# Attention's tiled products of a unit side by side, its transposes behind them; keys ahead of queries; routing and first-slot steps moved

## The chip, the cores and the metric

One core of one Trainium2 chip. The time is device microseconds of one execution of the whole program. Before the change three executions took 1027.92, 1023.63 and 1026.13 us, a median of 1026.13 us.

## What is computed

```python
# 1. chunked attention: 4 batches, 8 heads, 768 positions, head_dim 64; chunks of 32 queries
for c in range(24):
    k_full = concat(mem_k (8), k[c*32-16 : c*32+40])       # window clipped at the ends
    a = softmax(q[c*32 : c*32+32] @ k_full.T / 8)
    out[c*32 : c*32+32] = a @ v_full
# 2. mixture of 8 experts, the best one for each of the 3072 tokens (d = 512, f = 1024)
logits = x @ w_gate + modality_bias[modality_id];  e = argmax(logits);  gate = softmax(logits)[e]
out = gate * (relu(x @ w1[e]) @ w2[e])
# 3. a dense block: elu(x @ w_in) @ w_out, 512 -> 2048 -> 512
```

All in float32. Products of parts 2 and 3 are made of three products of split numbers (high and low parts).

## The kernel before, in words

The instructions of each engine stand in the order in which the Python program emits them (a manual schedule), so each engine is a queue: what stands first and waits holds up all behind it. PE is the matrix engine (TensorE), PEld its weight loads, DVE the VectorE, ACT the ScalarE, POOL the GpSimd, SP the engine that issues most transfers.

**Attention** (L54 to L515). An item is one batch and four heads (`items`, 8 of them); a unit is a third of an item, eight chunks (`units`, 24 of them, u = 3 ix + G). `A.run` (L442) emits for each unit: `sc(u, 0)` and `sc(u, 1)`, the scores of two groups of four chunks, in 32-column tiles (`tile_position`, L278); `sm(u)`, maximum and subtraction on DVE; `exp(u)` on ACT; `tr(u - 1)`, four 128 x 128 transposes of the unit before, and ACT's copy of them; `pv(u - 2)`, the products with v, again in 32-column tiles (L321), into one bank `ps_v`, from which DVE normalizes into x (L329). Beside them `step(i)` pops from `pend` the transposes that prepare the next item: `k_step` (three transposes, copies by ACT and DVE into `kbd`) and `q_step` (three transposes of `rl`, one copy by ACT into `qT`); `rl` is made by `relay` from the loaded q, on ACT up to item 3 and on POOL after. Three PSUM banks (`ps_t`) serve all transposes in turn. `load_v` and `load_qk` (SP) are issued at the first unit of an item; the halo of v is copied by POOL (`copy_v`).

The gate runs one batch behind: `gate_x` (eight transposes of x and two ACT copies), `gate_s` (x to the DRAM tensor xs, issued by POOL), `gate_l` (tiled products), `gate_t` (two transposes, a sum on DVE), `gate_e`, `gate_p`, `gate_r`, `gate_o` (choice of expert and ranks). `at(u, place, ...)` hangs them on places 0 to 5 of a unit; `side(u, place)` emits them. x and the staging of the memory's values (`repeat_v`, tensor mvd) share SBUF.

**Routing and slot 0.** The tokens of an expert are cut into slots of up to 384. Slot 0 needs batches 0 and 1 alone: `count`, `place`, `tokens(0)`, `gather(0)` (three indirect transfers issued by POOL), `scale` (ACT), `xT` (transposes). `M.first` (L891) runs slot 0's eight steps of `L1` (12 products) and, two steps later, `L2` (12 products), n = 2 to 9, with three places each, on which `program` hangs the last gates, `bases` (DVE), `slots` (POOL; it fills the register tile `reg`: which expert each slot has, how many slots there are), `tokens(1)`, `gather(1)` and `columns`. `split_w` makes high and low parts of a quarter of a pair of weight blocks (ACT casts, DVE subtracts); `load_w` brings a pair into one of three raw buffers. `M.run` (L910) then goes through slots 1 to 7 with PE as its pace, the rest of the slots follow under conditions, and `M2.run` is part 3.

Of the kernel before, what the change touches and what calls it, by code (L numbers as in the profile page):

```python
# [53 lines left out]
class Attention:  # L54
# [162 lines left out]
    def make_bias(self):  # L217

        nc, const, NT = self.nc, self.const, self.NT
        self.bias = self.rk.tile([128, NT, E], FP32, name="bias")  # L220
        tmp = const.tile([128, NT, E], FP32, name="btmp")
        mr = const.tile([NT, 128], FP32, name="mr")
        nc.vector.tensor_copy(out=mr, in_=self.mi[:, :, 0])
        mf = self.ps_t.tile([128, NT], FP32, name="ps_qk")
        nc.tensor.transpose(mf, mr, self.ident[0:NT, 0:NT])
        for m in range(2):
            m0 = const.tile([128, NT], FP32, name=f"m{m}")
            nc.vector.tensor_scalar(out=m0, in0=mf, scalar1=float(m), scalar2=None, op0=ALU.is_equal)
            o = self.bias if m == 0 else tmp
            nc.vector.tensor_tensor(out=o, in0=m0.unsqueeze(2).to_broadcast([128, NT, E]), in1=self.mb[:, m].unsqueeze(1).to_broadcast([128, NT, E]), op=ALU.mult)  # L230
        nc.vector.tensor_tensor(out=self.bias, in0=self.bias, in1=tmp, op=ALU.add)
# [26 lines left out]
    def tsteps(self, ix):  # L258
        steps = []
        for i in range(2):  # L260
            for j in range(2):
                steps.append(lambda i=i, j=j: self.k_step(ix, i, j))
                steps.append(lambda i=i, j=j: self.q_step(ix, i, j))
        return steps
# [177 lines left out]
    def run(self, more):  # L442
# [6 lines left out]
        def at(u, place, f, *a):  # L449
            todo.setdefault((u, place), []).append(lambda: f(*a))  # L450
# [5 lines left out]
        for b in range(self.B - 1):  # L456
            u0 = 6 * b + 6
            for G in range(3):
                at(u0 + G, 3, self.gate_x, b, G)
                at(u0 + G, 3, self.gate_s, b, G)  # L460
                at(u0 + G, 5, self.gate_l, b, G)
                at(u0 + G + 1, 2, self.gate_t, b, G)
# [10 lines left out]
        for u in range(N):  # L473
            ix, G = self.units[u]
            pops = [((0, 0, 0), (0, 0, 0), (3, 3, 2)), ((1, 1, 1), (1, 1, 1), (1, 1, 0))][ix > 0][G]
# [11 lines left out]
            if G == (2 if ix == 0 else 0) and ix + 1 < NI:  # L487
                self.relay(ix + 1, self.nc.scalar if ix < 3 else self.nc.gpsimd)
                pend = self.tsteps(ix + 1)
            self.sc(u, 0)  # L490
            side(u, 0)
            step(0)
            self.sc(u, 1)
            side(u, 1)
            if u:
                self.tr(u - 1)
            self.sm(u)
            side(u, 2)
            if u > 1:
                self.pv(u - 2)  # L500
            side(u, 3)
            step(1)
            self.exp(u)
# [5 lines left out]
            if u == 4:  # L509
                self.tables()  # L510
            if u == 5:
                self.make_bias()
# [33 lines left out]
class Routing:  # L546
# [139 lines left out]
    def slots(self):  # L686
# [34 lines left out]
        past(g1, base)  # L721
        TT(out=g1, in0=g1, in1=g2, op=ALU.subtract)
        self.g = g1
        eng.tensor_copy(out=reg[:, 2 * NSMAX:2 * NSMAX + 1], in_=end[:, 1, E - 1:E])
        eng.tensor_copy(out=reg[:, 2 * NSMAX + 1:], in_=base[:, 1, 0:1])
# [46 lines left out]
class Moe:  # L772
# [118 lines left out]
    def first(self, left):  # L891
# [6 lines left out]
        for n in range(LAG, NF + LAG):  # L898
# [5 lines left out]
            if n < 6:  # L904
                for i in range(2):
                    self.split_w(0, n // 2 + 1, 2 * (n % 2) + i)
# [252 lines left out]
def program(ctx, tc, q, k, v, mem_k, mem_v, mid, wg, mbias, w1, w2, w_in, w_out, out):  # L1159
# [11 lines left out]
    with ExitStack() as c2:  # L1171
        late, c4, c5, c6 = [ExitStack() for _ in range(4)]
        with tc.manual_schedule(engines=ORDER):
# [18 lines left out]
            def rest():  # L1192
# [4 lines left out]
                M.load_w(0, 3)  # L1197
# [14 lines left out]
                (N - 1, 2): [*[(M.split_w, 0, 1, i) for i in range(2)], (M.L1, 0, 0)],  # L1212
# [12 lines left out]
                (6, 0): [(rt.tokens, 1), (M.gather, 1), (rt.others, 2)],  # L1225
                (6, 2): [(rt.columns,)],
# [3 lines left out]
                (8, 2): [*[(M.xT, 1, kc) for kc in range(2, KC)]],  # L1230
# [81 lines left out]
```

## Time and profile before

| | us |
|---|---|
| median of three executions | 1026.13 |
| the profiled execution, its own time | 1027.93 |
| its span, first to last instruction | 1025.0 |
| PE busy | 976.8 (95% of the span) |
| DVE, ACT, POOL busy | 557.1, 426.8, 212.1 |
| mean granted clock of TensorE | 0.99 |

The rows below are from the page of the profile and from queries of its trace. Times in them are us from the start of the span unless ns stands there. A line number is that of the kernel before. Matmul ends are modelled, so durations of products overlap; the distance from start to start is what tells PE's pace.

### The profile page before, as it was taken

What the parts mean: (1) busy time and instruction counts of PE and PEld (TensorE: products, weight loads), DVE (VectorE), ACT (ScalarE), POOL (GpSimd) and SP (SyncE); (2) the same over time, 40 slices, a digit from 0 to 9 for tenths busy, and PEclk for the clock granted to TensorE, in tenths of its full rate; (3) what the DMA queues carried; (4) which work ended last, traced back from release to release, by engine and by line L of the source; (5) the groups of instructions that cost most, each with busy time, mean ns of one, the idle gap of its engine ahead of it and who ended that gap; (6) DMA issues with size and microseconds to landing.
All of it is one profiled execution on the core that took longest, in us unless ns stands there. A gap on an engine that the chain in (4) does not pass through costs nothing.

```text
span 1025.0 us, 17819 instructions
## 1 busy us (share of the span) xinstructions
PE 976.8 (95%) x7054; PEld 842.8 (82%) x7054; DVE 557.1 (54%) x1035; ACT 426.8 (42%) x782; POOL 212.1 (21%) x203
## 2 busy tenths in 40 slices
PE   3887888899999999998999999999999999999997
PEld 3766777899999999998878888888888888888886
DVE  3555767758999999655655334332433433343232
ACT  5665565266566556564444223222222322222221
POOL 7565640712342443210000100010010001001001
PEclk9899999999999999999999999999999999999999
DMA  9999861597987897764523101010110001001001
GB/s 218 179 206 210 161 206 43 146 350 253 326 323 266 307 348 268 245 201 160 163 85 122 42 1 42 1 42 0 42 42 1 1 1 42 1 0 42 1 1 41
DMA packets 94518, 131.29 MB, mean 128 GB/s; under 512 B 32251, under 2 KB 69197, under 8 KB 92377
## 3 DMA queue, kind: packets, MB, share of 16 engines
q1 hardware_dynamic: 83464, 98.11, 32.8%
q0 software_dynamic: 8816, 29.71, 8.8%
q10 hardware_dynamic: 2144, 2.23, 0.7%
q8 instruction: 59, 0.97, 0.4%
q14 instruction: 35, 0.28, 0.1%
HBM read 101.68 MB, written 28.35 MB: 127 GB/s over the span
## 4 chain that ended last, share of the span: by engine, by line
PE 51%; issue 35%; POOL 6%; DMA 4%; DVE 3%; SPq 1%; ACT 1%; POOLq 0%; ACTq 0%; DVEq 0%
PE b L877 13%; PE b L862 13%; PE b L1079 9%; PE b L1097 8%; POOL out_dram L1106 2%; DMA vw<-in_v_dram 1%; PE b L847 1%; PE b L278 1%; POOL vw L124 1%; PE b L321 1%; PE b L242 1%; DMA xs<-x 1%; DMA mk<-in_mem_k_dram 1%; PE b L346 1%; PE b L359 1%
## 5 line engine op out<-in xcount | busy, mean ns | idle before, releaser
L1084 DVE TENSOR_SCALAR g<-g 128x512 f32<-128x512 f32 x96 | 41.0, 428 | 251.1 <-ACT g L1083 251.1
L1083 ACT ACTIVATE g<-b 128x512 f32<-128x512 f32 x96 | 57.5, 599 | 264.8 <-PE b L1079 264.8
L1097 PE MATMUL b<-woh,gl 128*128 128x512 f32 x384 | 152.0, 396 | 0.0
L1097 PE MATMUL b<-woh,gh 128*128 128x512 f32 x384 | 152.0, 396 | 0.0
L1097 PE MATMUL b<-wol,gh 128*128 128x512 f32 x384 | 151.8, 395 | 0.0
L1106 POOL DMA_INDIRECT out_dram<-o,idc x24 | 23.4, 977 | 548.5 <-ACT o L1103 337.0
L1088 ACT CAST gh<-g 128x512 fp32r<-128x512 f32 x96 | 59.6, 621 | 117.4 <-DVE g L1085 116.2
L1079 PE MATMUL b<-c_xh,wih 128*128 128x512 f32 x384 | 105.4, 396 | 2.1 <-DMA x2T<-arena_vw 2.1
L1079 PE MATMUL b<-c_xh,wil 128*128 128x512 f32 x384 | 105.1, 395 | 0.8 <-issue 0.8
L1079 PE MATMUL b<-c_xl,wih 128*128 128x512 f32 x384 | 104.7, 395 | 0.0
L1089 DVE TENSOR_TENSOR gl<-g,gh 128x512 fp32r<-128x512 f32 x96 | 66.5, 693 | 65.9 <-ACT gh L1088 36.4
L877 PE MATMUL b<-hh,whi 128*128 128x384 f32 (+1 forms) x288 | 95.8, 332 | 0.8 <-ACT xT L347 0.8
L877 PE MATMUL b<-hl,whi 128*128 128x384 f32 (+1 forms) x288 | 95.5, 332 | 0.0
L877 PE MATMUL b<-hh,wlo 128*128 128x384 f32 (+1 forms) x288 | 95.3, 331 | 0.0
L826 DVE TENSOR_TENSOR wlo<-arena_ld,whi 128x512 fp32r<-128x512 f32 x128 | 85.5, 709 | 11.4 <-ACT whi L825 10.9
L1079 PEld LDWEIGHTS b<-c_xh,wih 128*128 128x128 f32 x384 | 72.6, 190 | 19.3 <-issue 2.3
L1079 PEld LDWEIGHTS b<-c_xh,wil 128*128 128x128 f32 x384 | 72.9, 190 | 17.6 <-issue 1.1
L1097 PEld LDWEIGHTS b<-wol,gh 128*128 128x128 f32 x384 | 72.2, 188 | 17.5
L1097 PEld LDWEIGHTS b<-woh,gl 128*128 128x128 f32 x384 | 72.2, 188 | 17.3
L1079 PEld LDWEIGHTS b<-c_xl,wih 128*128 128x128 f32 x384 | 72.7, 189 | 16.5
L1097 PEld LDWEIGHTS b<-woh,gh 128*128 128x128 f32 x384 | 72.1, 188 | 17.1
L825 ACT CAST whi<-arena_ld 128x512 fp32r<-128x512 f32 x128 | 72.7, 621 | 0.0
(254 smaller groups left out, 1656.8 us busy)
## 6 DMA issues: line engine op xcount, KB each, us to landing
arena_ld<-in_moe_w_dram SPq DMA_DIRECT2D x74, 512.0 KB
d<-in_moe_w_in_dram SPq DMA_DIRECT2D x8, 1024.0 KB
d<-in_moe_w_out_dram SPq DMA_DIRECT2D x8, 1024.0 KB
arena_ld<-in_k_dram SPq DMA_DIRECT2D x8, 768.0 KB
arena_ld<-in_q_dram SPq DMA_DIRECT2D x8, 768.0 KB
xs<-x POOLq DMA_DIRECT2D x12, 512.0 KB
x2T<-arena_vw SPq DMA_DIRECT2D x32, 192.0 KB
vw<-in_v_dram SPq DMA_DIRECT2D x12, 376.0 KB
```

Source lines behind the costliest of these rows:

```text
L124: eng.tensor_copy(out=run[p0 + CH:p0 + TOK, 0:2 * NC - 1], in_=run[p0:p0 + TOK - CH, 1:2 * NC])
L825: self.nc.scalar.copy(out=hi[:, c], in_=r)
L826: self.nc.vector.tensor_tensor(out=lo[:, c], in0=r, in1=hi[:, c].bitcast(FP32), op=ALU.subtract)
L862: nc.tensor.matmul(out=ps, lhsT=av[:, kc, 128 * r:128 * r + 128], rhs=b[:, kc, 0:N], start=n == 0, stop=n == 11)
L877: self.nc.tensor.matmul(out=self.acc[d][:, 0:self.N.get(s, SLOT)], lhsT=a[:, c:c + 128], rhs=b, start=f == 0 and i == 0, stop=f == NF - 1 ...
L1079: nc.tensor.matmul(out=ps, lhsT=a[:, kc, 128 * r:128 * r + 128], rhs=x[:, kc], start=n == 0, stop=n == 11)
L1083: nc.scalar.activation(out=g, in_=ps, func=ACTF.Exp)
L1084: nc.vector.tensor_scalar(out=g, in0=g, scalar1=1.0, scalar2=-1.0, op0=ALU.min, op1=ALU.add)
L1088: nc.scalar.copy(out=gh, in_=g)
L1089: nc.vector.tensor_tensor(out=gl, in0=g, in1=gh.bitcast(FP32), op=ALU.subtract)
L1097: self.nc.tensor.matmul(out=self.acc[t], lhsT=a[:, c], rhs=w[:, r], start=f == 0 and i == 0, stop=f == self.NF2 - 1 and i == 2)
L1106: ins = nc.gpsimd.indirect_dma_start(out=self.out, out_offset=bass.IndirectOffsetOnAxis(ap=self.idc[:, 4 * b + t:4 * b + t + 1], axis=0), ...
```

## The change

- `run` emits a unit's tiled products side by side: `gate_l` of the unit before (a new place -1), `sc(u, 0)`, `sc(u, 1)`, `pv(u - 2)`; then `tr(u - 1)` and all other transposes. `exp(u)` stands before the second `step`, and place 3 (`gate_x`, `gate_s`) behind it.
- `tsteps` lists an item's four key steps first, then its four query steps. They are popped as 3, 5 and 0 in the three units of an item (3, 3 and 2 before). For item 1 the relay stands behind two key steps.
- `make_bias` is cut in two: its first cast moves to the unit before.
- `slots` ends after the experts' register; the rest (`within`) moves behind `gather(1)`. `others(2)` moves one place back, `columns` from (6, 2) to (8, 2).
- Slot 0's splits: weight pair 3's first two halves move from n = 4 to n = 3, its last two from n = 5 to n = 7. `load_w(0, 3)` is emitted at the last attention unit.

```diff
-    def make_bias(self):
+    def make_bias(self, part):
         nc, const, NT = self.nc, self.const, self.NT
+        if part == 0:
+            self.mr = const.tile([NT, 128], FP32, name="mr")
+            nc.vector.tensor_copy(out=self.mr, in_=self.mi[:, :, 0])
+            return
...
     def tsteps(self, ix):
-        steps = []
-        for i in range(2):
-            for j in range(2):
-                steps.append(lambda i=i, j=j: self.k_step(ix, i, j))
-                steps.append(lambda i=i, j=j: self.q_step(ix, i, j))
-        return steps
+        return [lambda f=f, i=i, j=j: f(ix, i, j) for f in (self.k_step, self.q_step) for i in range(2) for j in range(2)]
...
-                at(u0 + G, 5, self.gate_l, b, G)
+                at(u0 + G + 1, -1, self.gate_l, b, G)
...
-            pops = [((0, 0, 0), (0, 0, 0), (3, 3, 2)), ((1, 1, 1), (1, 1, 1), (1, 1, 0))][ix > 0][G]
+            pops = [((0, 0, 0), (0, 0, 0), (4, 3, 2)), ((1, 1, 1), (2, 2, 1), (0, 0, 0))][ix > 0][G]
...
-                self.relay(ix + 1, self.nc.scalar if ix < 3 else self.nc.gpsimd)
                 pend = self.tsteps(ix + 1)
+                relay = lambda: self.relay(ix + 1, self.nc.scalar if ix < 3 else self.nc.gpsimd)
+                if ix == 0:
+                    pend.insert(2, relay)
+                else:
+                    relay()
+            side(u, -1)
             self.sc(u, 0)
+            self.sc(u, 1)
+            self.sm(u)
+            if u > 1:
+                self.pv(u - 2)
+            if u:
+                self.tr(u - 1)
             side(u, 0)
             step(0)
-            self.sc(u, 1)
             side(u, 1)
-            if u:
-                self.tr(u - 1)
-            self.sm(u)
             side(u, 2)
-            if u > 1:
-                self.pv(u - 2)
+            self.exp(u)
+            step(1)
             side(u, 3)
-            step(1)
-            self.exp(u)
             side(u, 4)
             step(2)
...
+            if u == 4:
+                self.make_bias(0)
             if u == 5:
-                self.make_bias()
+                self.make_bias(1)
...
         eng.tensor_copy(out=reg[:, 0:NSMAX], in_=small)
-        past(g1, base)
-        TT(out=g1, in0=g1, in1=g2, op=ALU.subtract)
+        self.g = g1, g2
+
+    def within(self):
...
+        eng.tensor_tensor(out=g1, in0=bs, in1=be, op=ALU.subtract)
+        eng.tensor_scalar(out=g1, in0=g1, scalar1=0.0, scalar2=None, op0=ALU.is_ge)
+        eng.tensor_tensor(out=g1, in0=g1, in1=g2, op=ALU.subtract)
         self.g = g1
...
-            if n < 6:
-                for i in range(2):
-                    self.split_w(0, n // 2 + 1, 2 * (n % 2) + i)
+            for fp, i in {2: [(2, 0), (2, 1)], 3: [(2, 2), (2, 3), (3, 0), (3, 1)], 7: [(3, 2), (3, 3)]}.get(n, []):
+                self.split_w(0, fp, i)
...
-                M.load_w(0, 3)
...
-                (N - 1, 2): [*[(M.split_w, 0, 1, i) for i in range(2)], (M.L1, 0, 0)],
+                (N - 1, 2): [*[(M.split_w, 0, 1, i) for i in range(2)], (M.L1, 0, 0), (M.load_w, 0, 3)],
...
-                (6, 0): [(rt.tokens, 1), (M.gather, 1), (rt.others, 2)],
-                (6, 2): [(rt.columns,)],
+                (6, 0): [(rt.tokens, 1), (M.gather, 1), (rt.within,)],
+                (6, 1): [(rt.others, 2)],
...
-                (8, 2): [*[(M.xT, 1, kc) for kc in range(2, KC)]],
+                (8, 2): [(rt.columns,), *[(M.xT, 1, kc) for kc in range(2, KC)]],
```

## Rows read from the trace of the kernel before

**Rows 1.** Table by stretches: length; busy us (count) per engine, clock, DMA share, GB/s.
```profile
147.10:199.76 52.66, 48.65 (x567) 43.04 (x565) 43.69 (x141) 22.30 (x46) 18.31 (x27) 1.00 0.29 78
199.76:211.40 11.64, 8.48 (x39) 7.93 (x38) 3.60 (x10) 5.18 (x10) 3.98 (x5) 0.71 0.67 198
211.40:480.00 268.60, 267.55 (x1634) 266.04 (x1632) 220.46 (x299) 162.92 (x311) 75.79 (x55) 1.00 0.81 283
```
**Rows 2.** Chain of work that ended last, around 60 to 72 us: start, length, what.
```profile
62.89 8.54 DMA xs<-x
71.52 0.76 DVE x L329 x2
```
**Rows 3.** Who waited for whom, PE, 72.3 to 147.1 us: total, times, longest.
```profile
PE b L278 <- issue: 6.0, 5, 2.4
PE b L406 <- DVE ohs L395: 1.9, 2, 1.0
PE b L242 <- POOL rl L237: 1.2, 1, 1.2
```
**Rows 4.** Table by stretches between ends of PE's stops, and their sum over eight.
```profile
75.77:83.90 8.13, 4.81 (x128) 3.97 (x127) 5.44 (x23) 4.42 (x9) 2.89 (x5) 1.00 1.12 206
...
90.69:97.43 6.74, 5.98 (x128) 4.65 (x127) 2.62 (x7) 4.46 (x9) 3.25 (x5) 1.00 1.00 332
...
110.01:122.11 12.10, 10.12 (x253) 8.36 (x257) 9.99 (x43) 6.50 (x14) 3.49 (x6) 1.00 0.69 157
...
sum 77.69, PE 66.22 PEld 52.76 DVE 46.94 ACT 44.85 POOL 45.65; mean PE 8.28 PEld 6.60 DVE 5.87 ACT 5.61 POOL 5.71
```
**Rows 5.** Instructions in order of time, PE: start, length, line, operation, [idle before].
```profile
59.32 0.66 PE L307 MATMUL b<-ident,p 128*128 128x128 f32 x4
59.81 0.38 PE L368 MATMUL b<-ident,ls 128*128 128x128 f32 x2
60.12 1.09 PE L321 MATMUL b<-vw,pt 128*32 128x130 f32 x32
61.15 1.09 PE L346 MATMUL b<-ident,x 128*128 128x128 f32 x8
...
150.58 0.66 PE L307 MATMUL b<-ident,p 128*128 128x128 f32 x4
151.16 1.09 PE L321 MATMUL b<-vw,pt 128*32 128x130 f32 x32
152.08 0.37 PE L278 MATMUL b<-kbd,qT 128*32 128x112 f32 x8
```
**Rows 6.** Instructions in order of time, PE and DVE, the first 33 us.
```profile
13.32 0.85 PE L242 MATMUL b<-ident,rl 128*128 128x128 f32 x3
14.73 0.55 PE L242 MATMUL b<-ident,rl 128*128 128x128 f32 x3
...
32.08 0.76 DVE L329 TENSOR_TENSOR x<-b,den 128x256 f32<-128x256 f32 x2 [0.26 <-DMA mvd<-x]
```
**Rows 7.** Instructions in order of time, ACT and PE, 144 to 155 us.
```profile
144.58 1.97 ACT L838 ACTIVATE arena_vw<-arena_vw 128x512 f32<-128x512 f32 x3
...
154.29 0.66 PE L307 MATMUL b<-ident,p 128*128 128x128 f32 x4 [1.03 <-ACT p L301]
```
**Rows 8.** The hand-over: DVE and POOL instructions, then the chain that ended last.
```profile
179.86 1.29 DVE L826 TENSOR_TENSOR wlo<-arena_ld,whi 128x512 fp32r<-128x512 f32 x2
...
189.94 1.31 POOL L720 CAST reg<-r_small 1x15 int32<-1x15 f32 x1
195.27 1.88 POOL L832 DMA_INDIRECT arena_vw<-xs,idx  x1 [0.16 <-issue]
...
202.80 0.73 ACT arena_vw L838
204.69 3.84 PE b L877 x12
209.43 2.10 PE b L877 x12
```

More of the change, by code (lines that the diff above doesn't have):

```diff
@@ L215, in tables @@
         routing_consts(nc, self.K)
-    def make_bias(self):
+    def make_bias(self, part):
         nc, const, NT = self.nc, self.const, self.NT
+        if part == 0:
+            self.mr = const.tile([NT, 128], FP32, name="mr")
+            nc.vector.tensor_copy(out=self.mr, in_=self.mi[:, :, 0])
+            return
+        mr = self.mr
         self.bias = self.rk.tile([128, NT, E], FP32, name="bias")
         tmp = const.tile([128, NT, E], FP32, name="btmp")
-        mr = const.tile([NT, 128], FP32, name="mr")
-        nc.vector.tensor_copy(out=mr, in_=self.mi[:, :, 0])
         mf = self.ps_t.tile([128, NT], FP32, name="ps_qk")
@@ L720, in slots @@
         eng.tensor_copy(out=reg[:, 0:NSMAX], in_=small)
-        past(g1, base)
-        TT(out=g1, in0=g1, in1=g2, op=ALU.subtract)
+        self.g = g1, g2
+    def within(self):
+        eng, end, (g1, g2) = self.nc.gpsimd, self.D["end"], self.g
+        bs = self.D["sl"].unsqueeze(2).to_broadcast([1, NSMAX, 2 * E])
+        be = self.base[0:1].rearrange("p s e -> p (s e)").unsqueeze(1).to_broadcast([1, NSMAX, 2 * E])
+        eng.tensor_tensor(out=g1, in0=bs, in1=be, op=ALU.subtract)
+        eng.tensor_scalar(out=g1, in0=g1, scalar1=0.0, scalar2=None, op0=ALU.is_ge)
+        eng.tensor_tensor(out=g1, in0=g1, in1=g2, op=ALU.subtract)
         self.g = g1
-        eng.tensor_copy(out=reg[:, 2 * NSMAX:2 * NSMAX + 1], in_=end[:, 1, E - 1:E])
-        eng.tensor_copy(out=reg[:, 2 * NSMAX + 1:], in_=base[:, 1, 0:1])
+        eng.tensor_copy(out=self.reg[:, 2 * NSMAX:2 * NSMAX + 1], in_=end[:, 1, E - 1:E])
+        eng.tensor_copy(out=self.reg[:, 2 * NSMAX + 1:], in_=self.base[0:1, 1, 0:1])
     def columns(self):
```

## The prediction

> **What bounds the kernel now.** I read the table by stretches first, then the chain of work that ended last, then TensorE's instructions and waits inside each stretch. The table [rows 1] cuts the span where the change stops and starts to matter. From 211.40 us on PE is busy 267.55 of 268.60 us, so what the kernel loses or wins before that point comes out at the end one for one; nothing of the change lies behind it. The change lies in three stretches: attention up to 147.10 us, the last attention units with slot 0 up to 199.76 (PE busy 48.65 of 52.66 us), and the hand-over to slot 1 up to 211.40, where PE is busy 8.48 of 11.64 us at a granted clock of 0.71.
>
> Attention itself is not held by one engine. Up to 71.5 us the chain goes through POOL and a transfer [rows 2]: POOL, after memsets, the tables and the copies of v, issues gate_s(0,0) only at 62.89, and its transfer takes 8.54 us; then DVE may overwrite x (L329, 71.52), and PE's pv(7) must wait for that write. After 72.3 us PE's waits [rows 3] are small but for one kind: 6.0 us of "issue" inside the score products (L278), in which no engine is waited for. The table between the ends of two such stops [rows 4] shows what they are: in 8.13 us PE issued 128 products and 127 weight loads, 255 instructions, and between two later ends of stops, 90.69 and 97.43, the same 255 in 6.74 us. 12.10 us later in attention hold 253 + 257, twice as many. I read this as the instruction stream coming in blocks of some 256, the next one asked for as one is begun and queued behind the bulk transfers (DMA share 1.12 and 1.00 in these two stretches, 0.69 in the third). A block costs the larger of PE's own pace and the supply.
>
> **The change part by part.** *Fewer changes between 32-column tiles and whole-array transposes.* Start to start, the four transposes of tr take 0.49 us when transposes follow (59.32 to 59.81) and 0.58 when tiled products follow (150.58 to 151.16); pv takes 0.92 us when scores follow (151.16 to 152.08) and 1.03 when transposes follow (60.12 to 61.15) [rows 5]. So a pair of changes costs 0.09 + 0.11 = 0.20 us. A unit had three pairs (scores, step, scores, tr, pv, steps); now it has one. That is 0.4 us per unit of PE's own pace, 8.4 us over the 21 units after the first three.
>
> *Up to 72.3 us: 0.* The POOL queue keeps its order (v_blocks, tables, copy_v, gate_s), so 71.52 stays, and pv(7) with it. Inside, make_bias's early cast and keys-first take PE waits away, but cover for later slips is needed too: in unit 2 pv(0)'s write of x waits for the mvd transfer until 32.08 us [rows 6], and the DVE halves of the first key copies now stand behind that write, with PE's fourth key step behind their bank, and unit 3's scores behind all. I put unit 3 some 1 us later than before, hidden by ACT's relay of item 3 and by the 71.52. If that cover were gone it would cost 1 to 4 us.
>
> *72.3 to 147.1 us: 1.0 us less.* Thirteen units at 0.4 are 5.2 us, and of the waits in [rows 3] gate_p's 1.9 (it now comes after scores, pv and tr) and the relay's 1.2 (three key steps need no relay) can go: 8.3 us if PE's pace were all, which is the far bound. But where the supply of instructions rules, a faster PE only waits longer; the five stops of [rows 3] are certain, I take three more blocks as just met, eight of the twelve, and there the two waits are worth nothing either. In the other four I keep some 0.4 each plus half the relay's wait, 2.2 us. Against that: steps now come as 3, 5 and 0 per item rather than 3, 3 and 2, so blocks are uneven (a unit without steps has 200 instructions in about 2.6 us and waits for the next block, the five-step unit is held by ACT's copies out of three banks), which I put at 0.7 us; and xT(0) at the end needs gather(0) scaled, 144.58 + 1.97 us [rows 7], a chain of tokens(0), POOL and a full DMA queue, which now starts behind two steps more. It lets through some 1 us at most. So 1.0, bounds +1.5 (the uneven blocks alone, twice) and -8.3.
>
> The Trainium skill ("Runtime: NRT & Kernel Launch", section "Instruction fetch mechanics") speaks against my reading: blocks of 256 instructions fetched while the current one runs, and the fetch hidden behind dispatch. The trace shows the blocks and not the hiding, by the 6.0 us. If the page held here, the middle would give the far bound; that is the second rival.
>
> *147.1 to 199.76 us: 1.2 us less.* In unit 23 tr(22) waited 1.03 us for its exponential [rows 7]; now pv(21), 0.92 us, stands in front of it. With two units' changes of mode, 0.8, the bound is -1.8; DVE, which has the weight splits here, may take all of it (0). I take two thirds.
>
> *The hand-over: 3.8 us less.* Slot 0's weight split of fp 3 moves: two halves earlier (n = 3), two later (n = 7). DVE does two splits in 1.29 us [rows 8], and these two now stand in front of bases, so bases, and slots on POOL, come 1.3 us later. But of slots the part called within goes behind gather(1): the register for the experts is done at 189.94 + 1.31 = 191.25, while the gather was issued at 195.27. So gather(1) comes 4.0 - 1.3 = 2.7 us earlier; its index is ready by then, as DVE has no splits at n = 4 and 5. Its last scaling ends at 200.8 instead of 203.5. PE comes there about 1.1 us later than 199.76, as tokens(1) waits for bases, so it hardly idles, and the half clock that followed the idle time (twelve products 3.84 us, not 2.10) goes: 1.7 us. 2.7 + 1.7 = 4.4, less 0.6 for the late splits at n = 7, whose casts now queue on ACT behind the scalings and in front of xT's. POOL's within (the 4.0 us) now stands in front of gather(2), which serves slot 2 and has a whole slot of time; columns, moved to n = 8, needs within, and nobody waits for columns before slot 1 is stored. Bounds: -1.4 (the clock falls all the same) and -5.9: in 11.64 us PE has 24 products (4.2) and 12 transposes (1.5) to do.
> load_w(0,3) only changes its place in SP's program: SP issues it when a ring buffer comes free, by the same split as before. 0.
>
> The sum: 0 - 1.0 - 1.2 - 3.8 = -6.0 us. The profiled execution took 1027.93 us (span 1025.0); it would give 1021.9. It lies 1.8 us over the median of the three runs shown, 1026.13, and against the median the forecast is 1020.1.
>
> **The rivals.** (a) *Only the hand-over pays, at its lower bound.* Supply, ACT and gather(0) take all of attention's gain back: -1.4, 1024.7. For it: eight supplied blocks, the 144.58. Against it: PE's pace does rule some blocks [rows 4].
> (b) *PE's own pace rules attention*, since the stops shrink with other transfers in flight: -8.3 - 1.8 - 3.8, about 1012. For it: DMA share under 0.7 after 110 us; against it: the stops at a share near 1.
> (c) *Slower: supply gets scarcer.* Scores, pv and scores of the next unit now run with hardly a transpose between, so PE asks for blocks in bursts. Twelve blocks took 77.69 us (the sum in [rows 4]), 6.5 each; if all take the 8.13 us of the worst, attention grows by 20 us. It beats the hand-over's 3.8 from 6.8 us per block on; at 7.3 it gives +9.9 - 3.8, about 1032.
> (d) *Slower: the clock.* With 20 to 30 transposes in a row the clock could fall in each unit. At the start three transposes took 0.85 us at the lower clock and 0.55 at the full one [rows 6]; for some 100 such groups that is +30 us, about 1050. Against it: in those rows the clock rose from 1.2 to 2.4 GHz while PE had done nothing but transposes. The rule is of the Trainium skill ("TensorE: Matmul & The Clock Gate", "Part 4: PE-mode transpose": transposes don't bring the full clock); the trace differs.
> (e) *The registers' move does nothing*, since gather(1) waits for its index instead: part of (a).
>
> **How the numbers follow.** Forecast 0.47, own range 1017 to 1024; (a) 0.25; (b) 0.18; (c) 0.08; (d) 0.02. About 0.5%, 5.1 us, is what a measurement of this kernel can tell from no change. Faster by more (under 1021.0): two thirds of the forecast's share and (b), 0.50. Slower by more (over 1031.3): (c) and (d), 0.10. Within: 0.40. The range for 8 in 10 runs from 1013, about half of (b), to 1027, all of (a); it leaves out some 0.19.
>
> **What would show it.** Right: PE still stops inside L278 every 255 instructions; DVE's first write after gate_s still starts near 71.5; gather(1) is issued near 191 to 193 counted from the same place of slot 0; PE idles under 1 us before xT(1) and the granted clock has no low stretch there; L1 of slot 1 starts near 205 instead of 211.4. Wrong: pv(7) well off 72.3 us (then the POOL chain was not the bound, or the start slipped); stops gone (b) or longer (c); a clock under 1.00 between 72 and 147 us (d); PE waiting at tokens(1) as long as it waited for the gather.

## The result and the profile after

The changed kernel takes 1034.9 us (median of 6 runs, 1033.2 to 1037.5), the kernel before 1026.0 beside it (1022.3 to 1028.6): a ratio of 1.0092, 95% interval 1.0064 to 1.0120. It is slower by some 9 us; forecast were 6 less. The profiled execution took 1037.1 us with a span of 1034.7, 9.7 more than before's 1025.0.

Where the 9.7 us came in, by marks that both traces have (us from the span's start):

| mark | before | after | difference | forecast by then |
|---|---|---|---|---|
| scores of unit 3 begin | 34.0 | 37.4 | +3.4 | some +1, hidden later |
| pv(7) begins | 72.3 | 73.9 | +1.6 | 0 |
| xT(0) begins | 147.1 | 155.5 | +8.4 | -1.0 |
| slot 0's L1, n = 2 | 167.0 | 175.8 | +8.8 | |
| slot 1's L1, n = 0 | 211.4 | 218.7 | +7.3 | -6.0 |
| slot 1's L1, n = 5 | 228.7 | 236.8 | +8.1 | -6.0 |
| end of the span | 1025.0 | 1034.7 | +9.7 | -6.0 |

So attention lost 8.4 us and the hand-over won far less than forecast. The last 1.6 us came behind 462 us, at the step from the experts to the dense block. From slot 1's n = 5 to the end, where their code is the same, the kernels of this document took 793.7 to 797.9 us (before 796.3, after 797.9), so I count it to none of the edits.

**Attention.** The waits of PE from pv(7) to xT(0), which answer [rows 3] (who waited for whom: total us, times, longest):

```profile
PE b L276 <- issue: 6.6, 5, 2.7
PE b L245 <- DVE kbd L259: 2.1, 2, 1.1
PE b L245 <- ACT kbd L259: 2.0, 4, 0.9
PE b L245 <- ACT qT L251: 1.5, 1, 1.5
PE b L319 <- DVE x L327: 1.3, 1, 1.3
PE b L357 <- ACT xT L345: 1.2, 2, 0.6
PE b L627 <- ACT kbd L259: 0.9, 1, 0.9
PE b L344 <- DVE kbd L259: 0.6, 1, 0.6
```

The stops inside the score products (L276 now) are still there, 6.6 us for 6.0. The six rows on kbd, qT and xT, 8.3 us, are waits of PE's next transposes or small products until ACT or DVE has copied an earlier group out of the three turning banks of PSUM; in the xT row gate_l waits for the copy itself. Before, rows of that kind came to 1.5 us in the same stretch. What such a wait looks like, in unit 18 (PE, then ACT: start, length, line, operation, [idle before <- releaser]):

```profile
132.50 0.66 PE L305 MATMUL b<-ident,p 128*128 128x128 f32 x4
132.99 0.82 PE L245 MATMUL b<-ident,arena_ld 128*128 128x128 f32 x6
133.65 0.60 PE L344 MATMUL b<-ident,x 128*128 128x128 f32 x4
134.88 0.66 PE L344 MATMUL b<-ident,x 128*128 128x128 f32 x4 [0.63 <-DVE kbd L259]
135.86 0.55 PE L245 MATMUL b<-ident,arena_ld 128*128 128x128 f32 x3 [0.33 <-ACT kbd L259]
136.47 0.90 PE L357 MATMUL b<-xT,wgp 128*32 128x256 f32 x6
```

```profile
133.25 0.59 ACT L307 COPY pt<-b 128x512 f32<-128x512 f32 x1 [2.30 <-PE b L305]
133.73 0.50 ACT L259 COPY kbd<-b 64x384 f32<-64x384 f32 x1
134.12 0.63 ACT L299 ACTIVATE p<-p 128x512 f32<-128x512 f32 x1
134.76 1.05 ACT L259 COPY kbd<-b 64x384 f32<-64x384 f32 x2
135.83 1.07 ACT L345 COPY xT<-b 128x512 f32<-128x512 f32 x2
136.79 0.56 ACT L259 COPY kbd<-b 64x384 f32<-64x384 f32 x1
```

From 132.50 on PE has 21 transposes in a row: tr's four, three key steps, gate_x's eight. ACT has to copy pt (0.59 us), four key halves (0.5 to 0.56 each) and xT twice (0.54 each) and to do the exponential (0.63), and runs without a gap from 133.25 to 137.3. PE issues a group of three in 0.33 us and is held at 134.88 and 135.86, and its gate_l at 136.47 comes no sooner than xT. Before, pv stood between tr and the next group [rows 5], and half of the unit's score products between two steps.

**The clock.** Table by stretches, pv(7) to xT(0) first, then two stops and what came behind each of them (length; busy us (count) of PE, PEld, DVE, ACT, POOL; clock, DMA share, GB/s):

```profile
73.90:155.46 81.56, 64.88 (x1492) 52.66 (x1484) 46.86 (x150) 43.09 (x88) 42.60 (x37) 0.96 0.80 185
78.25:81.30 3.05, 0.46 (x17) 0.32 (x18) 1.75 (x7) 0.81 (x3) 0.00 (x0) 1.00 0.78 268
81.30:85.00 3.70, 3.58 (x81) 3.17 (x81) 1.60 (x4) 0.00 (x0) 0.00 (x0) 0.54 0.06 20
91.50:94.60 3.10, 0.46 (x29) 0.28 (x19) 0.76 (x2) 0.68 (x2) 3.03 (x2) 1.00 0.90 109
94.60:98.60 4.00, 3.96 (x57) 3.52 (x58) 2.53 (x7) 0.91 (x2) 3.94 (x4) 0.58 0.93 290
98.60:155.46 56.86, 47.21 (x1097) 37.84 (x1095) 33.06 (x103) 33.88 (x70) 31.26 (x26) 1.00 0.77 195
```

Behind each of the two long stops PE ran at about half clock (0.54 and 0.58; 1.2 GHz is 0.50) for some 4 us; ahead of the first it had done 15 transposes and the start of the scores. After the stops of [rows 4] the clock stayed at 1.00. But the lower clock is no mark of the change: with the hand-over's edits alone (experiment 1), whose attention is that of before, a stop in the same place was followed by it, and pv took 1.96 us there, not 1.09 [rows 5]:

```profile
82.32 0.23 PE L278 MATMUL b<-memT,qT 128*32 128x16 f32 x1 [2.25 <-issue]
...
85.46 1.96 PE L321 MATMUL b<-vw,pt 128*32 128x130 f32 x32
```

From pv(7) to xT(0) the mean granted clock was 0.94 to 0.96 in three traces of before's attention (the hand-over's edits, the registers and the splits alone), 1.00 in before's own and 0.96 in the changed kernel's.

**The start.** The chain that ended last, around 17 to 34 us, answers [rows 2, 6]:

```profile
17.66 14.86 DMA mvd<-x
...
32.62 0.76 DVE x L327 x2
...
33.40 0.57 DVE kbd L259
...
34.02 0.92 PE b L245 x3
```

pv(0)'s write of x waits for the transfer into mvd until 32.62, DVE's key copy stands behind it, PE's key step behind that; PE did nothing from 28.2 to 34.0.

**Slot 0 and the hand-over.** The stretch from xT(0) to slot 1's first xT, then to slot 1's L1, answers [rows 1]; after that PE, DVE and POOL where they answer [rows 7, 8]:

```profile
155.46:210.84 55.38, 50.20 (x567) 44.61 (x566) 40.70 (x134) 24.04 (x49) 16.27 (x27) 0.97 0.30 82
210.84:218.69 7.85, 6.21 (x43) 5.44 (x39) 5.73 (x16) 2.92 (x8) 3.96 (x5) 1.00 0.44 119
218.69:487.00 268.31, 267.78 (x1629) 265.49 (x1630) 221.03 (x301) 162.49 (x310) 75.92 (x55) 1.00 0.82 286
```

```profile
163.44 1.09 PE L319 MATMUL b<-vw,pt 128*32 128x130 f32 x32 [1.55 <-ACT arena_whi L838]
...
198.24 1.80 PE L627 MATMUL b<-r_ja,pos 128*128 128x6 bf16 x24 [0.64 <-DVE r_ja L619]
199.90 0.94 PE L875 MATMUL b<-arena_xh,whi 128*128 128x384 f32 x4
200.68 1.13 PE L875 MATMUL b<-arena_xh,wlo 128*128 128x384 f32 x4
201.61 1.48 PE L875 MATMUL b<-arena_xl,whi 128*128 128x384 f32 x4
```

```profile
188.73 2.49 DVE L839 TENSOR_TENSOR wlo<-arena_ld,whi 128x512 fp32r<-128x512 f32 x4
```

```profile
199.74 0.19 POOL L725 CAST reg<-r_small 1x15 int32<-1x15 f32 x1
201.61 1.10 POOL L845 DMA_INDIRECT arena_vw<-xs,idx  x1 [1.68 <-DMA xs<-x]
```

The hand-over itself (first xT to L1 of slot 1) takes 7.85 us at a clock of 1.00; before it was 11.10 at 0.69, from the first xT at 200.30. But the stretch in front of it takes 55.38 us, not 53.20: four splits in one piece (2.49 us) stand in front of bases, PE waits 0.64 at tokens(1), and L1 behind it begins at the lower clock (four products 1.13 and 1.48 us, not 0.85). POOL had the experts' register at 199.93, but gather(1) waited a further 1.68 us for gate_s's transfer into xs.

### The profile page after: what moved, and what is told of

Same layout as the page of the kernel before. It is cut to its first block, busy times and chain, and to the rows that moved or that the text cites. A ratio compares the mean times of both kernels' runs of the same rounds, so it can differ in the third digit from the quotient of the medians.

```text
span 1034.7 us, 17819 instructions
## 1 busy us (share of the span) xinstructions
PE 975.7 (94%) x7054; PEld 843.0 (81%) x7054; DVE 556.9 (54%) x1035; ACT 425.2 (41%) x782; POOL 210.2 (20%) x203
## 4 chain that ended last, share of the span: by engine, by line
PE 53%; issue 35%; DMA 4%; DVE 3%; ACT 3%; POOL 2%; ACTq 0%; POOLq 0%; SPq 0%; DVEq 0%
PE b L875 14%; PE b L890 13%; PE b L1091 9%; PE b L1109 8%; PE b L276 2%; PE b L319 2%; POOL out_dram L1118 2%; DMA mvd<-x 1%; PE b L860 1%; PE b L245 1%; PE b L357 1%; DMA arena_ld<-in_q_dram 1%; PE b L305 1%; DMA x<-in_mem_v_dram 1%; DMA vw<-in_v_dram 1%
## 5 line engine op out<-in xcount | busy, mean ns | idle before, releaser
L879 ACT ACTIVATE hh<-b 128x384 fp32r<-128x384 f32 (+1 forms) x72 | 34.5, 479 | 93.0 <-PE b L875 92.4
```

Of the source, the lines that this page charges most:

```text
L879: nc.scalar.activation(out=hh, in_=ps, func=ACTF.Relu)
```

## The experiments

Four theories. **Theory 1, banks**: transposes side by side wait for the copies out of three banks; the tiled products that used to lie between them were the cover. **Theory 2, start**: the loss comes from the late start, from keys first. **Theory 3, supply**: instructions come later, or the clock falls behind the stops. **Theory 4** (formed after the first four runs), **DVE's order**: pv's write of x now stands in front of gate_t's reduction. All ratios are to the kernel before on the same chip, with 95% intervals; 0.1% is 1.03 us. The kernels ran on several chips, on which before's median was 1026.0 to 1027.2 us. Each kernel here, also those that compute with wrong values, has 7054 products on PE, so wrong values change no number of slots.

**1. The change in halves.** The hand-over's edits alone (slots, within, others, columns, the splits and load_w), then attention's alone.

> The kernel before with the hand-over's edits alone: within and others behind gather(1), columns at n = 8, slot 0's splits of fp 3 and load_w(0,3) in their new places; attention untouched. If the hand-over pays what the two traces show there (3.9 us from L1(0,7) to L1(1,0), less what the splits cost in slot 0), the time is 2 to 4 us less than before, and gather(1) is issued some 2.7 us earlier in slot 0. Rival (a transfer decides): gather(1) waits for gate_s's transfer into xs and not for its place on POOL; then it comes no more than 2 us earlier and the time is within 1 us of before. If the loss of the whole change were here, it would be 5 us or more slower.

> The kernel before with attention's edits alone: the new order in a unit, keys first with steps 3, 5, 0 (4, 3, 2 in item 0), gate_l one unit on, make_bias in two parts, the relay between the key steps; the hand-over untouched. If attention holds the whole loss: 9 to 13 us over before, more than the whole change, as the hand-over's gain is missing. If the loss is only in the hand-over or in slot 0: within 3 us of before.

Measured: 0.9998 (0.9965 to 1.0031) and 1.0104 (1.0052 to 1.0155). The whole loss is attention's, and the hand-over pays nothing that can be measured, though gather(1) did come 2.1 us earlier (26.2 us after slot 0's L1 at n = 2, before 28.3). POOL waited 2.06 us for gate_s's transfer there, as the rival said.

**2. Attention in two parts.** The order in a unit alone, and keys first with the new counts of steps alone:

```
 order:  sc(0) step(0) sc(1) tr sm pv step(1) exp step(2)        (before)
         sc(0) sc(1) sm pv tr step(0) exp step(1) step(2)        (order alone)
 steps:  k q k q k q k q, 3+3+2 per item -> k k k k q q q q, 3+5+0 (keys alone)
```

> The kernel before with the new order in a unit alone (scores of both halves, softmax, pv, tr, then steps and gate; gate_l one unit on); steps as before, key and query in turn, 3, 3, 2 per item. Theory 1 (banks): transposes that stand side by side wait for ACT and DVE to empty three banks of PSUM, since no tiled product lies between them any more: 3 to 7 us over before, with PE waits behind L259's, L251's and L307's copies. Theory 2 (start): the loss comes from keys first and the fourth key step of item 0, so this kernel is at before's time less up to 2 us. Theory 3 (supply): scores and pv in one run ask for blocks of instructions in bursts: 3 to 7 us over before, but as longer stops inside the score products, 10 us of them instead of 6.

> The kernel before with keys first and the new counts of steps alone (3, 5, 0 per item, 4, 3, 2 in item 0, relay between item 1's key steps), in the old order of a unit. Theory 1 (banks): the tiled products still lie between the steps, but five steps in one unit fall on the same banks: 1 to 4 us over before. Theory 2 (start): most of the 9 us is here, 5 us or more over before, with pv(0) and unit 3 late at 28 to 38 us. Theory 3 (supply): within 1.5 us of before.

Measured: 1.0096 (1.0066 to 1.0126) and 1.0019 (0.9994 to 1.0045). The order alone costs as much as the whole change; theory 2 has some 2 us, 4.6 at the end of the interval. In the trace of the order alone the stops inside the scores came to 1.1 us after pv(7), not 10, so theory 3 doesn't explain it. Two things stood out there. From pv(7) to xT(0) it took 79.4 us, 4.6 more than before, with PE's waits for copies at 10.8 us (before 1.5), in these rows above all:

```profile
PE b L278 <- ACT qT L248: 4.2, 2, 2.2
PE b L242 <- DVE kbd L256: 2.6, 3, 1.1
PE b L346 <- ACT kbd L256: 1.7, 2, 0.8
```

In the first row the scores wait for the copy itself, the queries; with gate_l's wait for xT, 1.2 us, that is half of the 10.8. In the others transposes wait for a bank. So "banks" stands for copies that come late in both ways; no run tried a fourth bank. Nor was the order taken apart from gate_l's place one unit on and exp's ahead of a step, which are part of it. And pv(7) itself came at 77.5 us, by this (PE, then DVE, of the order alone):

```profile
68.15 0.66 PE L346 MATMUL b<-ident,x 128*128 128x128 f32 x4 [0.82 <-ACT kbd L256]
73.68 1.12 PE L346 MATMUL b<-ident,x 128*128 128x128 f32 x4 [4.87 <-DVE L L371]
```

```profile
72.74 0.76 DVE L329 TENSOR_TENSOR x<-b,den 128x256 f32<-128x256 f32 x2 [5.78 <-DMA xs<-x]
73.41 0.21 DVE L371 TENSOR_REDUCE L<-b 128x16 f32<-128x64 f32 x1
```

pv(6)'s write of x (L329) waits 5.78 us for gate_s's transfer out of x, as in [rows 2]. Before, gate_t's reduction (L371) ran ahead of pv's; now it stands behind, and PE's gate_x waits 4.87 us for its bank. That is theory 4.

**3. The copies shortened.** The key and query steps' copies out of PSUM take 16 of 128 columns, so queries and keys are incomplete; PE's instructions stay the same.

```
-  cp(out=kv[:, :, :, r], in_=ps[half].rearrange("p s i -> p i s"))
+  cp(out=kv[:, 0:16, :, r], in_=ps[half].rearrange("p s i -> p i s")[:, 0:16])     (q likewise)
```

> The kernel before in which ACT's and DVE's copies out of the banks in the key and query steps take 16 of 128 columns (queries and keys are incomplete; two memsets of qT on DVE at the start stand in); PE's instructions are the same in number and order. It is the base for order_short. Theory 1 (banks): before already covers most of these copies with tiled products between the steps, so it gains little, 0 to 4 us. Theory 3 (supply): no change.

> The new order in a unit alone (order_only) with the same shortened copies of the key and query steps. Theory 1 (banks): transposes side by side wait for those copies; with the copies a fraction as long, the new order loses little or gains what the fewer changes of tile are worth: between 4 us less and 2 us more than before_short (order_only is 9 us more than before). Theory 3 (supply or clock): PE issues the same instructions in the same order, so the 9 us stay, 7 us or more over before_short.

Measured: 0.9984 (0.9965 to 1.0003) and 1.0042 (1.0019 to 1.0065): the order's price falls from 9 to some 5 us, more than the 2 that theory 1 alone allowed. The trace parts the two causes. From pv(7) to xT(0) it is now 74.6 us against 74.7: there nothing is left of the 4.6, and PE's waits for copies are 4.8 us, not 10.8. The rest is up to pv(7), where the wait for gate_t's reduction was 8.8 us this time (PE's waits of the order with short copies, 15 to 152 us):

```profile
PE b L348 <- DVE L L373: 8.8, 1, 8.8
```

**4. pv ahead of tr alone**, the steps still where they were, and **the same with gate_t moved forward**:

```
 sc(0) step(0) sc(1) sm pv tr gate_t step(1) exp step(2)         (pv first)
 sc(0) gate_t step(0) sc(1) sm pv tr step(1) exp step(2)         (gate_t forward)
```

> The kernel before with one step of the order alone: softmax's DVE part and pv(u-2) stand ahead of tr(u-1); the first steps of a unit still lie between its two score halves and the last ones behind tr. One pair of tile changes less per unit, 0.2 us each. Theory 1 (banks): score products and pv still cover the copies of the first step, but tr, gate_t and the second step now stand together: -3 to +2 us against before. Theory 4 (DVE's order: pv's write of x, which waits for gate_s's transfer, now stands ahead of gate_t's reduction on DVE and so of the next gate_x on PE): a wait of PE's gate_x for DVE of 2 to 5 us near 70 us, as in order_only, and +2 to +5 us.

> pv ahead of tr (pv_first) with gate_t's transposes and reduction moved ahead of softmax and pv, behind the unit's first scores. Theory 4 (DVE's order): pv_first lost 5 us since gate_t's reduction stood behind pv's write of x (PE waited 7.37 us there); this wait goes, and with one pair of tile changes less per unit the time is 1 us over to 3 us less than before. If pv ahead of tr costs by itself (its reads of pt, its bank): 3 us or more over before.

Measured: 1.0049 (1.0028 to 1.0071) and 1.0079 (1.0049 to 1.0109). The first is what theory 4 said: pv(7) at 77.8 us behind a wait of 7.37 us for gate_t's reduction, and from there to xT(0) 74.3 us, against 74.8 before: with score products still between the steps the stretch does not grow. Whether one pair of changes less pays can't be read from 0.5 us. The second is a miss. pv(7) comes at 71.7, so that wait is gone, but PE's gate_t now waits for ACT's copy of ls (2.4 us in four waits), waits for POOL's relay came to 5.2 us, and the stretch to xT(0) takes 79.1 us, in a profiled execution that was the fastest of six, 3.3 us under their median; I have no full account of that.

**5. The transfer earlier.** The order alone, with POOL's copy of v for item 2 behind gate_s(0,0) instead of in front of it:

```
-            if G == 2 and ix + 1 < NI:
+            if G == 2 and ix + 1 < NI and u != 5:
                 self.copy_v(ix + 1)            # and copy_v(2) at unit 6, behind side(u, 3)
```

> The new order in a unit alone (order_only), with POOL's copy of v for item 2 moved behind gate_s(0,0), so that this transfer of x into xs starts some 5 us earlier. Theory 4 (DVE's order): in order_only pv(6)'s write of x waited on DVE until 72.74 us for that transfer, gate_t's reduction stood behind it, and PE's gate_x behind that (4.87 us); with the transfer earlier this wait goes, pv(7) starts at 72 to 74 us instead of 77.5, and the time is 3 to 5 us less than order_only, 4 to 7 us over before (what is left is the waits for the banks after that). If the wait was only a place where other losses gathered: pv(7) earlier, but xT(0) as late as in order_only and the time within 1.5 us of it.

Measured: 1.0050 (1.0025 to 1.0076), 3.7 us less than the order alone by the medians, 4.7 by the two ratios. POOL issues the transfer at 57.49 us, not 63.44; pv(7) starts at 73.5, and DVE waits for no transfer there. From pv(7) on it takes 79.8 us, as the order alone did (79.4). So the order's 9 to 10 us are two prices of like size: about 4 by DVE's order and 4.6, by these traces, by the late copies.

**6. The registers' move without the splits, and the splits without the registers.**

> The kernel before with the registers' move alone (within and others behind gather(1), columns at n = 8); slot 0's splits of fp 3 stay. In the hand-over's edits together, bases came late behind the moved splits, PE waited 0.65 us at tokens(1) and a stretch of half clock cost some 1.6 us there. If those splits ate the gain: 1.5 to 3.5 us less than before, gather(1) at its full 2.7 us earlier, no low clock at tokens(1). Rival (the gain is not there, since something else is late next at slot 1's start, such as its weights' casts): within 1 us of before, L1 of slot 1 as late as in the hand-over's edits together.

> The kernel before with only slot 0's splits of fp 3 and load_w(0,3) in their new places; registers and columns as before. The registers' move alone gave 0.997 of before, both edits together 0.9998. If the splits give the gain back (bases late behind two more splits, PE waiting at tokens(1), half clock behind it, two casts late at n = 7): 1 to 4 us over before. If the two edits only hinder each other: within 1 us of before.

Measured: 0.9970 (0.9939 to 1.0000) and 1.0013 (0.9986 to 1.0040). From slot 0's L1 at n = 2 to slot 1's at n = 5, past the whole hand-over: before 61.7 us, registers alone 59.2, splits alone 62.0, both 60.9; the ten kernels with the hand-over untouched lie between 60.3 and 61.9. The first interval ends at no change, but experiment 9 repeats the gain with the same move. It comes otherwise than expected: gather(1) is issued 26.7 us after slot 0's n = 2, 1.6 earlier than before and not 2.7, as POOL waits for its index:

```profile
197.03 1.10 POOL L840 DMA_INDIRECT arena_vw<-xs,idx  x1 [2.37 <-DVE idx L629]
```

And the hand-over keeps a stretch at the lower clock: from the first xT to L1 9.3 us at 0.82, before 11.1 at 0.69. tokens(1) and the products behind it show what the splits cost (PE; registers alone, then splits alone):

```profile
192.00 1.64 PE L622 MATMUL b<-r_ja,pos 128*128 128x6 bf16 x24
193.50 0.94 PE L870 MATMUL b<-arena_xh,whi 128*128 128x384 f32 x4
194.28 1.00 PE L870 MATMUL b<-arena_xh,wlo 128*128 128x384 f32 x4
```

```profile
192.36 1.80 PE L622 MATMUL b<-r_ja,pos 128*128 128x6 bf16 x24 [0.64 <-DVE r_ja L614]
194.02 1.62 PE L862 MATMUL b<-arena_xh,whi 128*128 128x384 f32 x4
195.44 1.49 PE L862 MATMUL b<-arena_xh,wlo 128*128 128x384 f32 x4
```

With the splits in their new place PE waits 0.64 us at tokens(1), and the next products run at the lower clock (1.62 and 1.49 us for four; 0.94 and 1.00 without).

**7. Supply.** v is loaded for the first three items only (later items multiply old values), in the kernel before and in the changed one; and the changed one with short copies too, with all transfers and with few.

```
-  if i < NI:
+  if i < NI and (f != self.load_v or i < 3):
       f(i)
```

> The kernel before with v loaded for the first three items alone (later items multiply old values of v; the large transfers of attention fall by their largest part after some 45 us). The prediction's reading was that PE's stops inside the score products (6.0 us after 72.3 us, every 255 instructions) are instruction blocks queued behind these transfers, and that eight blocks of twelve go by supply. If so: the stops go, and 72.3 to 147.1 us shortens by 4 to 8 us unless POOL or DVE is late next. If the stops are of another kind: they stay, 5 us or more, and the time is within 2 us of before.

> The whole change with v loaded for the first three items alone, as in before_nov (1020.6 us, 72.0 us from pv(7) to xT(0)). If the whole change loses by the supply of instructions and the half clock behind its stops: stops and low clock between 74 and 150 us are gone and it comes within 2 us of before_nov. If it loses by the copies out of the banks: PE still waits 7 us or more for ACT and DVE there, 77 to 79 us from pv(7) to xT(0), and it stays 5 us or more over before_nov.

> The whole change with the key and query copies out of the banks taking 16 of 128 columns (queries and keys incomplete, as in before_short; two memsets of qT on DVE at the start). Theory 1 (banks): the changed kernel's 81.6 us from pv(7) to xT(0) fall to 74 to 76 us, since the five-step unit no longer waits for ACT; the time is 4 us or more less than the changed kernel, 1028 to 1031 us. If its loss is the clock after the stops, or the late start: 80 us or more there, and the time within 2 us of the changed kernel.

> The whole change with both taken away: v loaded for the first three items alone, and the key and query copies out of the banks 16 of 128 columns. If copies and supply together are the loss: 70 to 73 us from pv(7) to xT(0), and within 2 us of before_nov (1020.6), or below it by the fewer changes of tile. If it is still 4 us or more over before_nov, the loss lies elsewhere (the start, pv's write of x, the hand-over).

PE's waits, from pv(7) to xT(0): for copies (the rows on kbd, qT and xT) and stops (the rows on "issue"). The clock is the mean granted one of that stretch.

| | pv(7) to xT(0), us | for copies | stops | clock | whole kernel, us |
|---|---|---|---|---|---|
| before | 74.8 | 1.5 | 6.2 | 1.00 | 1026.0 |
| before, short copies | 74.7 | 0.7 | 1.7 | 0.92 | 1025.3 |
| changed | 81.6 | 8.3 | 6.6 | 0.96 | 1034.9 |
| changed, short copies | 79.7 | 2.1 | 10.8 | 0.93 | 1032.9 |
| before, few transfers | 72.0 | 1.5 | 0.5 | 0.98 | 1020.6 |
| changed, few transfers | 76.2 | 8.1 | 2.7 | 0.98 | 1029.0 |
| changed, few transfers, short copies | 71.7 | 3.5 | 4.1 | 1.00 | 1025.1 |

The stops inside the scores, with few transfers in the kernel before, then in the changed one with short copies too:

```profile
PE b L278 <- issue: 0.5, 2, 0.3
...
PE b L278 <- issue: 4.1, 5, 2.2
```

Before with few transfers is at 0.9944 (0.9919 to 0.9969); its stops after 72 us came to 0.5 us, not 6.0. That fits stops tied to the transfers but doesn't show it: with all transfers they came to 1.7 us with short copies and to none in experiment 4's first kernel, and in the changed kernels with few transfers 2.7 and 4.1 us stay. In either case, most of them gone doesn't save the change: it stays 8.4 us over before with few transfers, and PE's waits for copies are 8.1 us, so theory 3 isn't the cause of the loss. The short copies with all transfers were a miss (1.0056, 1.0031 to 1.0080): nearly all waits for copies were gone, but in its profiled execution (4.8 us over its median) PE stopped on "issue" instead, 10.8 us in the stretch, one stop 4.9 us long. Also pv(6) came at 64.7 us there, not 68.7, and PE then waited 5.6 us for gate_t's reduction, which is theory 4's wait: pv(7) came at 75.9, 2.0 later than in the changed kernel. With both away the stretch falls to before's length, 71.7 against 72.0. So the copies cost the changed kernel 4.5 us there (76.2 less 71.7; 3.9 by the two medians, on one chip). What the stops and the lower clock add with all transfers in flight, 2.6 by the same sums (6.8 less 4.2), is less than what traces of before's order differ by (74.4 to 78.5 us, see below). The time stays 4.5 us over before's with few transfers, where 2 at most were expected, so part of the loss lies elsewhere. The 4.1 us by which its span is still longer lie outside the stretch: 1.6 up to pv(7), with PE's wait for gate_t's reduction at 3.6, 1.2 from xT(0) to slot 1's n = 5, and 1.5 behind that, where no edit reaches.

**8. Even steps.** The changed kernel with 3, 3, 2 steps per item, keys first:

```
-  ((1, 1, 1), (2, 2, 1), (0, 0, 0))
+  ((1, 1, 1), (1, 1, 1), (1, 1, 0))
```

> The changed kernel with its steps spread as before (3, 3, 2 per item instead of 3, 5, 0; keys still first). From pv(7) to xT(0) the changed kernel takes 81.6 us, the new order with key and query in turn and even steps 79.4, before 74.8. If the uneven steps make the difference: 2 to 3 us less than the changed kernel, 79 to 80 us there. If keys first makes it (all three of a unit's steps on ACT, whose key copies come in two halves): within 1 us of the changed kernel.

Measured: 1.0063 (1.0042 to 1.0083), 2 to 3 us less than the changed kernel, with intervals that overlap (1.0064 to 1.0120 for the changed one). In its trace pv(7) to xT(0) takes 78.2 us, 3.4 less than the changed kernel; but pv(7) came at 79.4, since the units in front of it are shorter, reach the write of x sooner and wait 6.4 us for gate_t's reduction. In the changed kernel pv(6) comes so late (68.7 us) that its write, at 70.99, doesn't wait: the slip hid theory 4.

**9. A version under both.** The kernel before with the registers' move, and with gate_s(0,0) issued earlier:

> The kernel before with the registers' move (within and others behind gather(1), columns at n = 8) and with POOL's copy of v for item 2 behind gate_s(0,0), attention's order and slot 0's splits as before. If both waits were real: pv(7) starts at 69 to 71 us and not at 72.3, slot 1 some 2.5 us earlier counted from slot 0's start: 3 to 5 us less than before, faster than both kernels. If attention is held after 72 us by the supply of instructions and not by the start: 2 to 3 us less, as with the registers' move alone.

Measured: 0.9969 (0.9946 to 0.9992), 1024.7 us: 2 to 3 us faster than the kernel before and 10 to 12 faster than the changed one. That is no more than the registers' move gives alone; the earlier transfer gave nothing here. pv(7) came at 73.0, not at 69 to 71, and from there to xT(0) it took 78.5 us, with 8.5 us of stops (2.3 at 81 to 84, 3.1 at 143).

One caution on single traces: the four kernels with before's attention untouched show pv(7) at 71.5 to 75.7 us and 74.4 to 76.1 us from there to xT(0). And the profiled executions lie between 3.3 us below and 4.8 above their kernel's median. Experiment 9, where PE's order in attention is that of before too, takes 78.5 us there, by stops. So a length from one trace, taken alone, shows nothing under some 4 us; what is said above of late copies and of DVE's order rests on the rows of waits and on the ratios of whole kernels.

## Why the prediction was wrong, and where it was right

**What bounds the kernel.** Right as far as it went: what is lost up to slot 1 comes out at the end. With few transfers the kernel before loses its stops (6.0 to 0.5 us), as the reading has it, and the stretch shortens by 2.8 us only, as PE then waits longer for POOL's relay and, in gate_p, for DVE (6.5 us together, not 3.1). But the reading stays argued: that blocks of instructions come late is taken from the distance of 255 instructions alone, and the stops vary between none and 10.8 us with all transfers in flight.

**Fewer changes of tile (-5.2 us of PE's pace in the middle, of which 1.0 was to arrive).** This is the step that failed, by its sign: +6.8 in the changed kernel (81.6 us; 83.0 with attention's edits alone, 74.4 to 76.1 in the four traces of before's attention). The working counted what a tiled product between two groups of transposes costs PE (0.20 us a pair) and not what it is worth as cover for ACT's and DVE's copies. A unit needs a pt copy, two xT copies and three key or query copies, at 0.5 to 0.6 us each, and three banks to turn them in. Of the prediction's terms, "the five-step unit is held by ACT's copies out of three banks" was mis-sized, and put down to the steps alone: 0.7 us for it, with a bound of 1.5, where PE's waits for copies grew by 6.8 us (1.5 to 8.3). Most of that is the order's, with even steps: 10.8 us of such waits, and 4.6 us more in the stretch. The steps of 3, 5 and 0 add 2 to 3 us by the medians, which is not clear of noise. The gain may exist in part: PE's busy time in the stretch, at few transfers, falls from 63.2 us before to 60.8 in the changed kernel with short copies, but up to 1.7 of these 2.4 us can be the clock (0.98 and 1.00), and it arrives as nothing while an engine beside it is late.

**Up to 72.3 us: 0.** POOL kept its order, as the step said: gate_s is issued at 62.92, not 62.89. The step missed what else is queued on DVE behind the write that waits for this transfer. The order puts gate_t's reduction there, and that made PE wait 3.6 to 8.8 us in the seven traces of such an order in which pv(6) came at 63 to 66 us. In the changed kernel the start had slipped 3.4 us, not the 1 us that was assumed, so the wait hardly showed, +1.6 at pv(7). The cover by ACT's relay and gate_s, which the step named, held for half of the slip.

**147.1 to 199.76 us: -1.2.** tr(22)'s wait of 1.03 us [rows 7] is gone, as forecast. But pv(21) in unit 23 waits 1.55 us, put down to ACT's cast of a weight split, which the step didn't look at, and with the late bases the stretch became 2.2 us longer.

**The hand-over: -3.8.** The mechanism of the gather was right. Counted from L1 at n = 2, gather(1) is issued after 25.8 us, not 28.3: 2.5 earlier, 2.7 forecast. Registers alone give 2.5 us of time against before's trace, 2.2 by the medians, though gather(1) comes only 1.6 earlier there. The step that failed is the clock behind the moved splits: the prediction let tokens(1) wait for bases (PE "comes there about 1.1 us later") and put no price on that in its sum. PE waited 0.64 us at tokens(1), and the half clock of the hand-over, whose 1.7 us were booked as gain, reappeared there, as the step's own bound of -1.4 has it. In the changed kernel gather(1) waited a further 1.68 us for gate_s's transfer into xs, a rival that the prediction lacked. Net of all, 0.8 us to slot 1's n = 5, and 61.0 us there is also what attention's edits alone took, without the hand-over's.

**The rivals.** (a) needed attention to lose nothing, (b) to gain. (c), supply, forecast a slower kernel, about 1032, by another mechanism, so its nearness to 1034.9 is luck: blocks did not get slower on the whole (6.6 us of stops for 6.0), and with most of the stops gone the loss stayed. (d) had the clock fall with transposes in rows; in the changed kernel's middle it fell behind stops only, in two stretches of 7.7 us with PE busy 7.5, so at most half of that, 3.8 us, is its price here, and traces of before's attention pay the like. The Trainium skill ("TensorE: Matmul & The Clock Gate", "Part 4: PE-mode transpose") has transposes not bring the full clock. With tiled products around them the run can't show that; they did not take it away: it stood at 1.00 for 56.86 us, with 21 transposes in a row in the midst. (e) holds in part: with the registers moved alone gather(1) waits 2.37 us for its index, and yet the registers' move is the one part that pays.

**Open.** Why the clock fell behind a stop of 2.25 us in one trace of before's attention and not behind 2.42 in another; how far a fourth bank would go; and why gate_t ahead of the steps lost 4.8 us after pv(7).

## What to carry to other kernels

Before products of one kind are put together to save an engine's own switching, list what the other engines drain while the products in between run, and how many buffers the drain has: 0.4 us a unit was to be saved on TensorE, and copies of 0.5 us out of three banks cost more. When an instruction that can wait for a transfer is moved on an in-order queue, price what now stands behind it and who waits for that. An edit that brings a late step forward is best tried without its neighbours: the registers' move alone was worth some 2 to 3 us and lost it to splits moved with it.

## What the runs showed of the hardware

PE's stops on "issue", where it waits for nothing that the profile shows, move with everything else: 6.0 us after 72 us in the kernel before, none between 72 and 100 us with the registers moved, one of 4.9 us at 147 with short copies. After two stops of 2.7 us the granted clock was 0.54 and 0.58 over some 4 us. It was at the lower level behind a stop of 2.25 us with the hand-over's edits alone too, and stayed at 1.00 behind one of 2.42 in the kernel before, with the same instructions. Small products after a wait of 0.64 us (24 of six columns at tokens(1)) were followed by a stretch at the lower level as well.
